# Two loads of v moved in a fused sigmoid attention and gated feed-forward kernel

## The chip, the cores and the metric

The kernel runs on one core of one Trainium2 chip. The metric is device time in microseconds (us) of one execution; the time given is the median of several runs. One further execution is recorded by the hardware profiler, and all views of the profile come from that one.

## The reference

The inputs are q, k and v of shape (8, 12, 448, 64) in float32 (batch, heads, sequence, head dimension), two weights of 768 x 1536 and one of 1536 x 768. Attention uses a sigmoid in place of the softmax, and its output, with heads joined, is the input of a gated feed-forward layer.

```python
scores = scale * np.matmul(q, k.transpose(0, 1, 3, 2)) - np.log(S)
attn = 1.0 / (1.0 + np.exp(-scores))
x = np.matmul(attn, v)                     # then heads joined: (3584, 768)
gate = np.maximum(x @ w_gate, 0.0)
out = (gate * (x @ w_val)) @ w_out
```

## The kernel before

All matrix work is in float16. For each batch the 12 heads are taken as three groups of four (g = 0, 1, 2). A batch passes through these steps:

- *Loads.* `load(b, g0, g1, "kq")` (L106, issued on L110) brings k and q, and `load_v(b)` (L112) brings v, converted from float32 to float16 on the way. They are issued from POOL (GpSimd), which carries out its instructions in order. v is three DMAs: one for the even head pairs (L114) and one for each half of the odd ones (L116), whose partitions are swapped. k and q of a batch have a single buffer (batch 1 has one of its own), v has two that alternate.
- *Transposes of k and q.* Batches 0 and 1 use TensorE (`pe_transposes`). From batch 2 on `dma_transposes(b, g)` (L211) is used: VectorE copies k and q of a group into `rel` (L215), and SyncE issues one DMA transpose from `rel` to `qkT` (L219).
- *Scores.* `qk_unit(b, g, c)` multiplies (L232), and ScalarE applies the sigmoid (L187) into `PT`.
- *pv.* `pv_group(b, g)` multiplies `PT` by v (L250), 28 matmuls for a group; VectorE writes the result to `xT` (L184).
- *Feed-forward.* `gv` forms gate and value for one block f of 128 columns of the two weights (L309), and `down` and `down_pair` multiply by the third weight (L346, L385). From the second half of the kernel on, pairs of batches and blocks are multiplied by a scheme with sums on VectorE and fewer products (`gv_pair`, `down_pair`).

The order on each engine is written out by hand. A loop over the batches (b = 1 to 7) cuts the 21 scores units of a batch into five or six stages (m). Between the scores units of a stage stand the pv groups, and after them a portion of feed-forward work of an earlier batch. Things that are to be issued in the middle of that portion are put in a list `jobs`, in order. So the scores and pv of batch 3 run between feed-forward work of batches 0 to 2, and the pv of a batch's first group is in its third stage (m = 2) from batch 2 on, and in its fourth (m = 3) in batch 1.

`hold(b, g)` (L645) is a copy of two elements of `qkT` on POOL. It computes nothing that is used: POOL can't go on before the DMA transpose (b, g) has landed, so the loads behind it are issued only then. Before the change there are two: on (2, 1), ahead of batch 2's v and the third weight (`late_loads`), and on (3, 2), ahead of batch 4's loads.

The opening loads are in one list (L132 to L160), cut into parts by group and by weight blocks: `load_gv(f0, f1)` loads blocks f0 to f1 - 1 of gate and value weights, one DMA each (L148). A load on POOL waits for the landing of the load eight places ahead of it.

Of the kernel before, what the change touches and what calls it, by code (L numbers as in the profile page):

```python
# [17 lines left out]
def kernel(  # L18
# [75 lines left out]
    def tiles_of(b):  # L94
        if b not in in_tiles:
            pool = early if b == 1 else inp
            in_tiles[b] = tuple(
                p.tile([P, NPAIR, NCH * D], FP16, tag=t, name=t)
                for p, t in ((pool, "k16"), (pool, "q16"), (vinp, "v16"))
            )  # L100
        return in_tiles[b]

    def rows_of(src, b):
        return src[b].rearrange("(x r) (t c) d -> (r t) x (c d)", r=2, c=NCH)

    def load(b, g0, g1, which, c0=0, c1=NCH):  # L106
        for nm, t16, src in zip("kq", tiles_of(b), (k, q)):
            if nm in which:
                xs, cs = slice(2 * g0, 2 * g1), slice(c0 * D, c1 * D)
                nc.gpsimd.dma_start(t16[:, xs, cs], rows_of(src, b)[:, xs, cs])  # L110

    def load_v(b):  # L112
        v16 = tiles_of(b)[2]
        nc.gpsimd.dma_start(v16[:, 0::2, :], rows_of(v, b)[:, 0::2, :])  # L114
        for r in range(2):
            nc.gpsimd.dma_start(  # L116
                v16[64 - 64 * r : P - 64 * r, 1::2, :], rows_of(v, b)[64 * r : 64 * r + 64, 1::2, :]
            )
# [25 lines left out]
    def load_gv(f0, f1, which=(0, 1)):  # L144
        fs = slice(f0 * P, f1 * P)
        for i in which:
            wt, src = ((wg, moe_w_gate), (wv, moe_w_val))[i]
            nc.gpsimd.dma_start(wt[:, :, fs], src[:, fs].rearrange("(c p) f -> p c f", p=P))  # L148
# [6 lines left out]
    load(1, 0, 1, "kq")  # L155
    load_gv(6, 9)
    load(1, 1, 2, "kq")
    load_gv(9, 12)
    load_v(1)
    load(1, 2, 3, "kq")  # L160

    def load_o():
# [27 lines left out]
    def qkT_of(b, g):  # L190
        if (b, g) not in qkT_tiles:
            qkT_tiles[(b, g)] = qkTp.tile([P, TW, P], FP16, tag="qkT", name="qkT")
        return qkT_tiles[(b, g)]
# [17 lines left out]
    def dma_transposes(b, g):  # L211
        k16, q16, _ = in_tiles[b]
        rel = relp.tile([P, TW, P], FP16, tag="rel", name="rel")
        for ti, t16 in enumerate((k16, q16)):
            nc.vector.tensor_copy(  # L215
                rel[:, ti * NCH : (ti + 1) * NCH, :].rearrange("p c (h d) -> p h c d", h=2),
                t16[:, 2 * g : 2 * g + 2, :].rearrange("p h (c d) -> p h c d", c=NCH),
            )
        nc.sync.dma_start_transpose(  # L219
            qkT_of(b, g)[:], rel[:].rearrange("p c x -> p (c x)")  # L220
        )
# [70 lines left out]
    def qk_unit(b, g, c):  # L292
        ps = [bank("qk_ps") for _ in range(2)]
        qk(qkT_tiles[(b, g)], c, 0, NCH, lambda hh: ps[hh][:, 0:S])
        PT = PTp.tile([P, 2, S], FP16, tag="PT", name="PT")
        for hh in range(2):
            sigmoid(PT[:, hh, 0:S], ps[hh][:, 0:S])
        PT_tiles[(b, g, c)] = PT

    def pv_group(b, g):  # L300
        pv(b, g, 0, S, [PT_tiles.pop((b, g, c))[:, :, 0:S] for c in range(NCH)])
# [66 lines left out]
    def open_late():  # L368
        first_sbuf.close()
        pool = ctx.enter_context(tc.tile_pool(name="late", bufs=1))  # L370
        late["T"] = pool.tile([P, 4, HF, HM], FP16, tag="T", name="T")
        late["X"] = pool.tile([P, 3, HD, S], FP16, tag="X", name="X")
        late["sums"] = ctx.enter_context(tc.tile_pool(name="sums", bufs=2))
# [21 lines left out]
    def weight_sums(i):  # L395
        T = [late["T"][:, j] for j in range(4)]
        B11, B21 = wo[:, 0:HF, 0:HM], wo[:, HF:NFC, 0:HM]
        B12, B22 = wo[:, 0:HF, HM:DM], wo[:, HF:NFC, HM:DM]
        sub(T[i], *((B12, B11), (B22, T[0]), (B22, B12), (B21, T[1]))[i])
# [96 lines left out]
    def batch_sums_t1(g):  # L496
        T1, _, _, B11, _, B12, _ = batch_blocks(g, (0, HD))
        sub(T1, B12, B11)

    def batch_sums(g, ks):  # L500
        T1, T2, T4, _, B21, B12, B22 = batch_blocks(g, ks)
        sub(B12, B22, B12)
        sub(T2, B22, T1)
        sub(T4, B21, T2)
# [132 lines left out]
    def pv_finish(b):  # L637
        pv_group(b, NG - 1)
        if b < 2:
            push_gv(b, 0, S, range(NFC))  # L640
# [4 lines left out]
    def hold(b, g):  # L645
        nc.gpsimd.tensor_copy(gate[0:1, :], qkT_tiles[(b, g)][0:1, 0, 0:2])

    def both(b, g):
        pe_transposes(b, g, 0)
        pe_transposes(b, g, 1)  # L650
# [10 lines left out]
    def push_group(g):  # L661
        tail = [("t", g, 6)] + [("y", g, p) for p in range(3)]
        if g == 0:
            tail.insert(0, tail.pop(1))
        work.extend([("w", g, f) for f in range(0, NFC, 2) if g > 0] + tail)
# [26 lines left out]
    for b in range(1, B):  # L692
        if b == 1:
            cuts, pv_at = (0, 3, 6, 9, 13, 17, 21), {3: (0, 2), 5: (1, 2)}
        elif b == 2:
            cuts, pv_at = (0, 4, 7, 11, 14, 18, 21), {0: (-1, 2), 2: (0, 2), 4: (1, 2)}
        else:
            cuts, pv_at = (0, 4, 8, 12, 16, 21), {0: (-1, 2), 2: (0, 2), 4: (1, 2)}
        count = len(cuts) - 1
        hooks = {}  # L700
        if b == 1:
            mix = (3, 3, 3, 3, 3, 2)
            hooks = {
                1: [(1, lambda: both(1, 1))],
                3: [(1, lambda: both(1, 2))],
                4: [(3, lambda: dma_transposes(2, 0))],
                5: [(2, late_loads)],
            }
        elif b == 2:
            mix = (2, 2, 1, 1, 1, 2)  # L710
            hooks = {
                2: [(0, prepare)],
                4: [(0, lambda: weight_sums(0))],
                5: [(1, lambda: weight_sums(1)), (0, lambda: weight_sums(2))],
            }
            open_late()
        elif b == 3:
            mix = (1, 1, 1, 0, 0)
        else:
            mix = (0,) * count  # L720
        for m in range(count):
            jobs = []
            for i, (g, c) in enumerate(order[cuts[m] : cuts[m + 1]]):
                if m in pv_at and i == pv_at[m][1]:
                    if m == 0:
                        pv_finish(b - 1)
                        if b == 2:
                            push_group(0)
                        elif b % 2 == 0:
                            push_group(b // 2 - 1)  # L730
                    else:
                        pv_group(b, pv_at[m][0])
                qk_unit(b, g, c)
            if m == 0 and b > 1:
                jobs.append(lambda: dma_transposes(b, 2))
            if b == 2 and m == count - 1:
                jobs.append(lambda: (dma_transposes(3, 0), dma_transposes(3, 1)))
            elif b == 3 and m == count - 1:
                jobs.append(lambda: (dma_transposes(4, 0), dma_transposes(4, 1)))
            elif 0 <= m - count + 2 and 3 < b < B - 1:  # L740
                jobs.append(lambda: dma_transposes(b + 1, m - count + 2))
            if b == 1:
                if m == 0:
                    load(2, 0, 1, "kq")
                    load(2, 1, 2, "kq")
                    load(2, 2, 3, "kq")
            elif m == 0 and b + 1 < B:
                if b == 3:
                    jobs.append(lambda: hold(3, 2))
                jobs.append(lambda: (load(b + 1, 0, 3, "kq"), load_v(b + 1)))  # L750
            if b % 2 and b > 2:
                if m == count - 1:
                    jobs.append(lambda: (batch_sums_t1(b // 2), batch_sums(b // 2, (0, 1))))
            elif b > 3 and m == 0:
                jobs.append(lambda: batch_sums(b // 2 - 1, (1, HD)))
            if b == 2 and m == count - 1:
                ffn_mix(mix[m], hooks[m])
                next_work(jobs + [lambda: weight_sums(3)], first_act=True)
            elif mix[m]:
                for job in jobs:  # L760
                    job()
                ffn_mix(mix[m], hooks.get(m, ()))
            else:
                next_work(jobs)
            if b == 3 and m in (1, 3):
                for f in range(*((0, 8, 2), (8, NFC, 2))[m // 2]):
                    gate_sums(f, f + 2)
# [35 lines left out]
```

## Time and profile before

| what | value |
|---|---|
| median of 3 runs | 398.85 us (397.96 to 398.97) |
| the profiled execution | 399.14 us |
| its span, first to last instruction | 397.3 us |
| PE (TensorE matmul) busy | 388.5 us, 98% |
| VectorE, ScalarE, POOL busy | 279.6, 223.2, 49.5 us |
| loads from POOL | 23.33 MB on one queue, as written |
| DMA transposes and stores | 19.34 MB on the SyncE queue |

A line of a timeline gives the start of a piece of work and its length in us, the engine, the line of the kernel, the operation with output and input, and how many instructions are merged; in brackets stands the idle time of the engine before it and what ended that. A line of the waits gives the total, the number and the longest. A line of DMA issues gives the size and the median time from issue to landing. A line for a queue gives packets, MB, and the time its packets took as a share of 16 DMA engines in the stretch that was asked for; q0 holds the loads that POOL issues, q1 what SyncE issues.

### The profile page before, as it was taken

The numbers are of one execution on the slowest core, as the hardware profiler recorded it, in microseconds if no ns is written. First come the engines' busy times: TensorE is split into PE (matmuls) and PEld (weight loads), VectorE is DVE, ScalarE is ACT, GpSimd is POOL, SyncE is SP. The second block draws the span as 40 slices with busy tenths as digits, with TensorE's granted clock in tenths as the row PEclk, the third lists the DMA queues.
The fourth block names the chain that finished last, engine by engine and source line by source line (L and its number), as shares of the span: only waits on it lengthen the run. The fifth ranks groups of instructions, "written<-read, shape, count | busy, mean of one in ns | idle before, by whom it ended". The sixth has DMA issues, their size and how long they took to land.

```text
span 397.3 us, 8744 instructions
## 1 busy us (share of the span) xinstructions
PE 388.5 (98%) x3488; PEld 217.5 (55%) x3488; DVE 279.6 (70%) x539; ACT 223.2 (56%) x476; POOL 49.5 (12%) x73
## 2 busy tenths in 40 slices
PE   8999999999999999999999999999999999999995
PEld 3678686445455554554555555455455555555563
DVE  3453345358377889999758889999776779987662
ACT  5946768684785565655665455565566233543121
POOL 8643400700030300003000300000000000000000
PEclk9999999999999999999999999999999999999999
DMA  9999994999999893224945695222013320000135
GB/s 150 196 198 204 206 129 87 180 203 190 203 143 180 167 218 53 46 48 54 177 84 133 130 219 89 48 21 57 19 40 81 81 79 2 0 1 2 40 94 146
DMA packets 68953, 43.69 MB, mean 110 GB/s; under 512 B 35888, under 2 KB 65584, under 8 KB 68912
## 3 DMA queue, kind: packets, MB, share of 16 engines
q0 software_dynamic: 30736, 23.33, 39.2%
q1 hardware_dynamic: 37744, 19.34, 23.2%
q8 instruction: 27, 0.44, 0.4%
q10 hardware_dynamic: 432, 0.46, 0.4%
q14 instruction: 14, 0.11, 0.1%
HBM read 47.19 MB, written 11.01 MB: 146 GB/s over the span
## 4 chain that ended last, share of the span: by engine, by line
PE 84%; DMA 11%; POOL 2%; ACT 1%; issue 0%; DVE 0%; ACTq 0%; POOLq 0%; DVEq 0%
PE u L385 32%; PE g L385 15%; PE y L385 8%; PE qk_ps L232 7%; PE pv_ps L250 7%; PE g_ps L309 5%; PE v_ps L309 5%; DMA wg<-in_moe_w_gate_dram 4%; DMA v<-in_v_dram 3%; PE ya L346 3%; DMA q<-in_q_dram 2%; PE yb L346 1%; DMA qkT<-rel 1%; ACT PT L187 1%; POOL k L110 1%; POOL q L110 1%
## 5 line engine op out<-in xcount | busy, mean ns | idle before, releaser
L187 ACT ACTIVATE PT<-qk_ps 128x448 f16<-128x448 f32 (+3 forms) x318 | 150.5, 595 | 72.6 <-PE qk_ps L232 72.5
L385 PEld LDWEIGHTS <-S 128*128 128x128 f16 x540 | 52.8, 98 | 43.6
L536 DVE TENSOR_TENSOR gsb<-g,gsb 128x448 f32<-128x448 f32 x72 | 42.9, 625 | 14.6 <-PE g L385 14.1
L232 PE MATMUL qk_ps<-qkT 64*64 64x448 f16 (+2 forms) x756 | 49.9, 336 | 1.3 <-DVE qkT L206 0.5
L421 ACT ACTIVATE ysb<-u 128x384 f32<-128x384 f32 x27 | 13.4, 498 | 53.4 <-PE u L385 53.4
L327 DVE TENSOR_TENSOR hT<-gate_sb,v_ps 128x256 f16<-128x256 f32 (+2 forms) x36 | 16.2, 465 | 34.7 <-ACT gate_sb L318 22.3
L532 ACT COPY gsb<-u 128x448 f32<-128x448 f32 x48 | 25.7, 566 | 23.9 <-PE u L385 22.9
L250 PE MATMUL pv_ps<-PT,v 64*64 64x448 f16 (+2 forms) x756 | 37.7, 329 | 1.1 <-DMA v<-in_v_dram 0.8
L184 DVE TENSOR_SCALAR xT<-pv_ps 128x448 f16<-128x448 f32 (+2 forms) x53 | 27.9, 567 | 15.2 <-PE pv_ps L250 13.8
L385 PEld LDWEIGHTS <-hT 128*128 128x128 f16 x288 | 27.7, 98 | 19.8 <-issue 2.1
L232 PEld LDWEIGHTS <-qkT 64*64 64x64 f16 x756 | 20.0, 105 | 25.5 <-issue 16.3
L309 PE MATMUL v_ps<-xT,wv 128*128 128x256 f16 (+2 forms) x216 | 33.3, 290 | 0.3 <-DMA wv<-in_moe_w_val_dram 0.3
L309 PE MATMUL g_ps<-xT,wg 128*128 128x256 f16 (+2 forms) x216 | 33.5, 291 | 0.1
L385 PEld LDWEIGHTS <-wv 128*128 128x128 f16 x216 | 21.1, 98 | 19.7
L385 PEld LDWEIGHTS <-wg 128*128 128x128 f16 x216 | 20.3, 98 | 20.6 <-issue 3.0
L250 PEld LDWEIGHTS <-v 64*64 64x64 f16 x756 | 21.8, 107 | 12.8 <-DMA v<-in_v_dram 1.5
L385 PE MATMUL u<-T,hT 128*128 128x384 f16 x144 | 27.3, 326 | 0.0
L437 DVE SCALAR_TENSOR_TENSOR ysb<-y,ysb 128x384 f32<-128x384 f32 x24 | 13.4, 557 | 17.8 <-PE y L385 10.3
L309 PEld LDWEIGHTS <-wg 128*128 128x128 f16 x216 | 18.5, 98 | 11.5 <-issue 5.0
L110 POOL DMA_DIRECT2D k<-in_k_dram x14 | 10.9, 780 | 110.7 <-DVE rel L215 104.4
L309 PEld LDWEIGHTS <-wv 128*128 128x128 f16 x216 | 20.1, 98 | 7.9 <-DMA wv<-in_moe_w_val_dram 0.6
L385 PE MATMUL u<-xT,wg 128*128 128x448 f16 x108 | 23.5, 353 | 0.1
(69 smaller groups left out, 531.0 us busy)
## 6 DMA issues: line engine op xcount, KB each, us to landing
out_dram<-ysb SPq DMA_DIRECT2D x52, 192.0 KB, 3.0
k<-in_k_dram POOLq DMA_DIRECT2D x5, 672.0 KB, 11.7
q<-in_q_dram POOLq DMA_DIRECT2D x5, 672.0 KB, 14.9
v<-in_v_dram POOLq DMA_DIRECT2D x8, 336.0 KB, 15.4
v<-in_v_dram POOLq DMA_DIRECT2D x16, 168.0 KB, 15.2
k<-in_k_dram POOLq DMA_DIRECT2D x8, 224.0 KB, 10.4
wo<-in_moe_w_out_dram POOLq DMA_DIRECT2D x1, 1536.0 KB, 13.1
q<-in_q_dram POOLq DMA_DIRECT2D x6, 224.0 KB, 11.3
```

The costliest lines, as they stand in the source:

```text
L110: nc.gpsimd.dma_start(t16[:, xs, cs], rows_of(src, b)[:, xs, cs])
L184: nc.vector.tensor_scalar(out=xT, in0=src, scalar1=XSCALE, scalar2=None, op0=AOP.mult)
L187: nc.scalar.activation(PT_ap, ps_ap, AF.Sigmoid, bias=sig_bias, scale=qk_scale)
L232: nc.tensor.matmul(out_of(hh)[o : o + 64, :], qkT[rows, c, cols], qkT[rows, NCH + c0 : NCH + c1, cols], start=True, stop=True, tile_positi ...
L250: nc.tensor.matmul(ps[hh][64 * r : 64 * r + 64, 0:qn], v16[rows, 2 * g + hh, c * D : (c + 1) * D], pieces[c][rows, hh, :], start=(c == 0), ...
L309: nc.tensor.matmul(ps[-1][:, 0:qn], wt[:, dc, f * P : (f + 1) * P], xT_tiles[b][:, dc, q0 : q0 + qn], start=(dc == 0), stop=(dc == NDC - 1),)
L327: nc.vector.tensor_tensor(out=hT_tiles[g][:, f, o : o + qn], in0=gate_sb[:, 0:qn], in1=ps[1][:, 0:qn], op=AOP.mult,)
L346: nc.tensor.matmul(ps[:, 0 : m1 - m0], hT_tiles[g][:, f, t * P : (t + 1) * P], wo[:, f, m0:m1], start=(f == 0), stop=(f == NFC - 1),)
L385: nc.tensor.matmul(ps[:, 0:n], A[:, k_, :], W[:, k_, :], start=(first and k_ == 0), stop=(k_ == kn - 1), skip_group_check=True,)
L421: nc.scalar.activation(o, ps[:, 0:HM], AF.Copy, scale=OUT_SCALE)
L532: by(gs[u][i][:], ps[u][:, 0:S])
L536: nc.vector.tensor_tensor(out=gs[u][i][:], in0=ps[u][:, 0:S], in1=gs[u][i][:], op=AOP.add)
```

## The change

Two loads change place. In the opening list batch 1's v is issued ahead of the gate and value weights of blocks 9 to 11 instead of behind them. Batch 3's v was issued right behind batch 3's k and q, in batch 2's first stage; it is now issued at the end of batch 2's last stage, after the first two DMA transposes of batch 3 and behind a new `hold(3, 1)`. For the later batches v stays behind k and q. No arithmetic changes.

```diff
     load(1, 0, 1, "kq")
     load_gv(6, 9)
     load(1, 1, 2, "kq")
+    load_v(1)
     load_gv(9, 12)
-    load_v(1)
     load(1, 2, 3, "kq")
...
             if b == 2 and m == count - 1:
-                jobs.append(lambda: (dma_transposes(3, 0), dma_transposes(3, 1)))
+                jobs.append(lambda: (dma_transposes(3, 0), dma_transposes(3, 1), hold(3, 1), load_v(3)))
...
             elif m == 0 and b + 1 < B:
                 if b == 3:
                     jobs.append(lambda: hold(3, 2))
-                jobs.append(lambda: (load(b + 1, 0, 3, "kq"), load_v(b + 1)))
+                jobs.append(lambda: (load(b + 1, 0, 3, "kq"), b > 2 and load_v(b + 1)))
```

## The prediction

> **What bounds the kernel now.** I read the page first: PE is busy 98% of the span, all 40 slices of the granted clock read 9, and the chain that ended last is 84% PE. So only time in which PE stands still can be won, and nearly any new PE wait is lost for good. PE's list of waits is next (who waited for what: us in total, times, longest):
>
> ```profile
> PE pv_ps L250 <- DMA v<-in_v_dram: 0.8, 2, 0.5
> PE qk_ps L232 <- DMA qkT<-rel: 0.4, 1, 0.4
> ```
>
> Both places are touched by the change. PE's timeline shows the first, at batch 1's first pv group (start, length, then the idle time in brackets):
>
> ```profile
> 47.18 0.35 PE L250 MATMUL pv_ps<-PT,v 64*64 64x448 f16 x2
> 47.83 0.37 PE L250 MATMUL pv_ps<-PT,v 64*64 64x448 f16 x1 [0.29 <-DMA v<-in_v_dram]
> 48.69 1.51 PE L250 MATMUL pv_ps<-PT,v 64*64 64x448 f16 x25 [0.49 <-DMA v<-in_v_dram]
> 49.85 0.72 PE L232 MATMUL qk_ps<-qkT 64*64 64x448 f16 x8
> ```
>
> The group holds PE from 47.18 to 49.85, 2.67 us; the next such group takes 1.32 in the chain. The wait costs 1.35 us. The second place and the pv group that needs batch 3's v:
>
> ```profile
> 101.36 0.57 PE L232 MATMUL qk_ps<-qkT 64*64 64x448 f16 x8 [0.45 <-DMA qkT<-rel]
> 101.76 1.49 PE L250 MATMUL pv_ps<-PT,v 64*64 64x448 f16 x28
> ...
> 109.47 0.57 PE L232 MATMUL qk_ps<-qkT 64*64 64x448 f16 x8
> 109.88 1.71 PE L250 MATMUL pv_ps<-PT,v 64*64 64x448 f16 x28
> ```
>
> Batch 3's pv starts at 109.88 with no wait, 8.5 us after the transpose wait. Then POOL's timeline, since POOL issues every load in order and its one-element copies (L646) hold it until a transpose has landed:
>
> ```profile
> 69.35 0.17 POOL L646 COPY gate<-qkT 1x2 f16<-1x2 f16 x1 [19.70 <-DMA qkT<-rel]
> 69.83 0.76 POOL L114 DMA_DIRECT2D v<-in_v_dram  x1 [0.31 <-issue]
> 70.58 1.25 POOL L116 DMA_DIRECT2D v<-in_v_dram  x2
> ```
>
> This is batch 2's v behind a hold, the nearest row for what batch 3's v becomes. Asked issue by issue, the DMA view gives time to landing: 5.4 us for each of these, so the last lands at 71.2 + 5.4 = 76.6, 6.8 us after the first issue.
>
> **Part 1, v1 ahead of the last weights.** Nothing is added; five DMAs change order. POOL's waits show that every load waits for the one eight places before it, so the issue slots stay at 26.34, 28.30, 29.44, 30.62 and 34.91. Today weights of blocks 9 to 11 take the first two and v the rest. Landings in that view follow the issue order: the second part of batch 1's q 40.0, wg 42.34, wv 45.2, v 46.9, 47.8 and 48.65. So in the steady stream wg takes 2.3, wv 2.86, v 3.45 us. Swapped: v lands at 40.0 + 3.45 = 43.45, 3.7 us before PE asks. wg lands at 45.8, wv at 48.65. Block 9 reads wg at 51.83 and wv at 52.49 now, so at 50.5 and 51.1 with the wait gone: spare 4.7 and 2.5 us. The k and q loads behind see the same bytes ahead of them; batch 1's last k and q land at 49.7 and 50.9 and are asked for at 51.9 and 52.3. Batch 2's first k and q land at 52.0 and 53.2, against copies at 54.3 and 54.6. ACT idles 1.4 to 1.8 us at 50 and 54, so it is not late next. Part 1 gains **1.35 us**, and all that hangs on PE after it moves forward by as much, the hold at 69.35 and the loads behind it included. From here I keep the clock of before, so this 1.35 is taken off once.
>
> **Part 2, batch 3's transposes without v3 under them.** v3 now lands at 97.4, 98.5 and 99.2, under the transpose issued at 96.75, which takes 4.56 us. The undisturbed ones of this trace take 3.9 to 4.1. With v3 gone it lands at 100.85 and the wait at 101.36 (0.45) goes; next late is PE itself, whose down product ends there anyway. The transposed copies can't start earlier: batch 3's q lands at 95.8, copied at 96.30. Gain **0.45**.
>
> **Part 3, v3 behind the hold.** Added: a hold on the transpose (3,1), 0.17 us of POOL; the three v issues move from 75.63 to behind it. Queued behind on POOL: the hold on (3,2), then batch 4's k, q, v. SP's queue is not reordered, but its next transpose, (3,2), issued at 105.11, now runs beside v3. When does (3,1) land? Now at 99.06 + 4.2 = 103.26. Batch 4's pair, alone, takes from 124.55 to 131.1, 6.55 us; from 96.75 that is 103.3. Same. As at 69.35 the first v issue follows 0.5 us later: **103.85**; the last ends near 105.9. PE asks at 109.88 - 0.45 = **109.43**, so 5.6 us are to be had. Landing has two bounds:
>
> - Alone, 6.8 us (batch 2's v): 110.65, a stall of 1.2.
> - Beside a transpose, bounded by the loads of k that share with one. At 183.8 the two are issued together, and the view answers, beside batch 4's k at 109.86:
>
> ```profile
> k<-in_k_dram POOLq DMA_DIRECT2D x1, 672.0 KB, 11.7
> qkT<-rel SPq DMA_TRANSPOSE x1, 11.5
> ...
> k<-in_k_dram POOLq DMA_DIRECT2D x1, 672.0 KB, 7.1
> ```
>
> k there has v's size (336 + 2 x 168 = 672 KB). The other two shared cases, at 133.6 and 225.3, took 9.9 and 11.8. The queues show why: in the two microseconds from 188 the load queue moved 0.27 MB beside the transpose's, against 0.40 alone from 75:
>
> ```profile
> q0 software_dynamic: 297, 0.27, 91.2%
> q1 hardware_dynamic: 294, 0.08, 40.5%
> ...
> q0 software_dynamic: 453, 0.40, 123.8%
> ```
>
> Which bound? Loads begin to flow 1.8 to 2.1 us after issue, so v3 at 105.8; transpose (3,2), issued at 104.65 by the earlier PE, flows from 105.9. They overlap fully, so the shared rows are the nearest. I take the shortest, 9.9, since only 672 KB run beside the transpose: 113.75, a stall of **4.3 us**; the ends are 1.2 and 115.65 - 109.43 = 6.2. No gain is possible here, as pv doesn't wait for v3 now.
>
> By the Trainium skill, "DMA: Bandwidth & Descriptors", section "Anatomy of one DMA", a load takes about 2.0 us plus its bytes over 436 GB/s. By that, an estimate, 0.69 MB would land 3.6 us after issue, before PE asks, with no stall and a sum of -1.8. The measured 5.4 and 7.1 stand against it, and I go by them.
>
> **What waits behind.** (3,2) lands late too, by 115 at most if it finishes with v3's tail. Its first qk runs at 114.9 + 3.85 = 118.7: free. Batch 4's loads start about 5.4 later (109.86 to 115.3): k lands at 122.4, q at 125.7, v at 129.4. The copies for batch 4 go from 123.80 to 127.65, its first transpose flows from 129.6: free, by little. PE has no slack later that could give the stall back.
>
> **Sum.** -1.35 - 0.45 + 4.3 = +2.5, between -0.6 and +4.4 by the bounds. On the profiled execution (span 397.3, 399.14 in all) that is 401.6; on the median 398.85, which lies 0.3 below it, **401.3**. A difference under 0.3%, 1.2 us, is no change here.
>
> **A clock that drops.** The longest idle of PE after the start is 0.49 us, so no row shows a 4 us one. Bounds from rows: nothing, or what the start shows, where ten 128x448 matmuls took 3.83 us, 0.38 each, against 0.19 later (six in 1.14): 1.9 us. I take nothing, as nearer to all 40 slices at 9, and keep 1.9 for a rival.
> "TensorE: Matmul & The Clock Gate", section "Part 1: The HAM clock gate", says that about 3.4 us of idleness can halve the clock. A 4.3 us stall would pass that mark, and by the rule the sum would be about 1.7 us higher; no row here shows it.
>
> **The rivals.**
> - *Faster: v3 arrives in time.* If (3,1), issued at 98.3 behind the quicker (3,0), lands 4.0 later, at 102.3, and v3 runs as batch 2's did, it lands at 109.65. Only 0.2 of stall is left: -1.6, 397.2. It decides from a landing of v3 before 110.0. For it: the issue of (3,0) takes 2.13 us now, 1.5 elsewhere. Against: the pair at 124.55, and three shared loads. 0.14.
> - *No change: a stall of about 1.2*, v3 ahead of the transpose on the engines. Sum -0.6, 398.3. Against: both flow from 105.8. 0.20.
> - *Part 1 does nothing:* wv, now last, is late at 51.1 instead. It would have to slip by 2.5. Sum +3.85, 402.7. 0.04.
> - *The clock drops* in the stall: +4.4, 403.3. 0.09.
>
> **Numbers.** My forecast has 0.53, of which 0.04 falls within 1.2 us. Slower: 0.49 + 0.04 + 0.09 = 0.62; same 0.20 + 0.04 = 0.24; faster 0.14. The forecast's own range is 399.5 to 403.2. The range for 8 in 10 takes in the no-change rival below and the longest stall above: 398.0 to 403.4.
>
> **What would show it.** Right: no v wait at pv near 47; the qk wait near 101 gone; POOL held until about 102 (all times 1.35 earlier), v issued just behind; a PE wait of 3 to 6 us for v at the pv near 108; shared landings of 9 us or more for v3, and transpose (3,2) above its 4.1. Wrong: landings of v3 under 7 us, a pv there without a wait, a new wait for wv near 51, or one for q or transposes near 128.

## The result, and the profile after

The changed kernel takes 403.63 us (median; 402.76 to 403.67) against 398.77 for the kernel before beside it: ratio 1.0123, 95% interval 1.0107 to 1.0139. It is slower by 4.9 us. The forecast was 401.3 with a range up to 403.4: the direction and the stall came as forecast, the size did not.

The profiled execution took 403.67 us with a span of 401.9. PE's waits in it (total, times, longest):

```profile
PE pv_ps L250 <- DMA v<-in_v_dram: 3.3, 3, 1.6
...
PE pv_ps L250 <- issue: 1.2, 1, 1.2
```

The wait for the transpose (3,0) is gone. The v wait is still there, but it has moved from batch 1 to batch 3. PE's timeline has both places:

```profile
48.23 1.49 PE L250 MATMUL pv_ps<-PT,v 64*64 64x448 f16 x28
49.55 0.55 PE L232 MATMUL qk_ps<-qkT 64*64 64x448 f16 x8
...
100.59 0.57 PE L232 MATMUL qk_ps<-qkT 64*64 64x448 f16 x8
101.00 1.49 PE L250 MATMUL pv_ps<-PT,v 64*64 64x448 f16 x28
...
110.34 0.38 PE L250 MATMUL pv_ps<-PT,v 64*64 64x448 f16 x2 [1.06 <-DMA v<-in_v_dram]
111.41 0.37 PE L250 MATMUL pv_ps<-PT,v 64*64 64x448 f16 x1 [0.69 <-DMA v<-in_v_dram]
113.36 2.81 PE L250 MATMUL pv_ps<-PT,v 64*64 64x448 f16 x25 [1.58 <-DMA v<-in_v_dram]
115.61 0.94 PE L232 MATMUL qk_ps<-qkT 64*64 64x448 f16 x8
116.48 1.31 PE L309 MATMUL g_ps<-xT,wg 128*128 128x448 f16 x6
```

The three waits of batch 3's group are its three DMAs, landing one after another. By the distance of 8.12 us from the pv group ahead of it in the trace of before, this one should have begun at 109.12 and its fourth matmul at 109.27; it ran at 113.36. The stall is **4.1 us**. What comes behind is slow too: the last 25 matmuls and the next eight take 3.12 us to the first g_ps, and 1.82 in a run further down in which the clock held. PE's granted clock, microsecond by microsecond (the column ahead of the last two; 1.00 is full speed, and up to 112 it reads 1.00):

```profile
112.00:113.00 1.00, 0.00 (x0) 0.00 (x0) 0.23 (x1) 0.00 (x0) 0.00 (x0) 0.81 1.29 188
113.00:114.00 1.00, 0.64 (x8) 0.37 (x12) 0.00 (x0) 0.00 (x0) 0.00 (x0) 0.50 0.89 164
114.00:115.00 1.00, 1.00 (x16) 0.50 (x12) 0.00 (x0) 0.00 (x0) 0.18 (x1) 0.50 0.09 16
115.00:116.00 1.00, 1.00 (x20) 0.42 (x13) 0.14 (x1) 0.00 (x0) 0.56 (x1) 0.50 0.03 8
116.00:117.00 1.00, 1.00 (x12) 0.43 (x5) 1.00 (x2) 0.54 (x2) 1.00 (x2) 0.98 0.00 0
```

The clock is halved from 112.6, still inside the stall, to 116.0. From 113.36 on PE has work and does it at half speed for 2.7 us: another **1.3 us**. The chain of waits names where v's time went, from the hold to the landing of the third DMA:

```profile
103.16 0.75 POOL v L114
103.91 0.62 POOL v L116
104.53 8.79 DMA v<-in_v_dram
113.32 0.04 issue
113.36 2.81 PE pv_ps L250 x19
```

From the first issue to the last landing are 10.16 us. And the transpose (3,2) that shares the engines, in SP's timeline, takes 5.26 us to issue where it took 1.55 before the change, and lands 10.0 us after its start, not 4.1:

```profile
104.45 5.26 SPq L219 DMA_TRANSPOSE qkT<-rel  x1
```

PE's place against the trace of before, whose matmuls behind batch 3's first pv start so:

```profile
111.89 1.31 PE L309 MATMUL g_ps<-xT,wg 128*128 128x448 f16 x6
```

Step by step: +1.05 us at batch 1's first pv (the pause near 22 us is longer, 1.15 against 0.27), -0.30 behind it, -0.77 at batch 3's first scores, +4.59 behind batch 3's first pv, and no more after that; the span grew by 4.6.

### The profile page after: what moved, and what is told of

It reads as the page before. It is cut to its first block, busy times and chain, and to the rows that moved or that the text cites. A ratio compares the mean times of both kernels' runs of the same rounds, so it can differ in the third digit from the quotient of the medians.

```text
span 401.9 us, 8747 instructions
## 1 busy us (share of the span) xinstructions
PE 390.6 (97%) x3488; PEld 218.2 (54%) x3488; DVE 279.6 (70%) x539; ACT 223.3 (56%) x476; POOL 49.8 (12%) x74
## 3 DMA queue, kind: packets, MB, share of 16 engines
q0 software_dynamic: 30736, 23.33, 39.5%
## 4 chain that ended last, share of the span: by engine, by line
PE 93%; ACT 3%; DMA 2%; issue 1%; DVE 1%; POOL 0%; ACTq 0%; DVEq 0%
PE u L385 32%; PE g L385 15%; PE y L385 9%; PE qk_ps L232 9%; PE pv_ps L250 8%; PE g_ps L309 7%; PE v_ps L309 6%; PE ya L346 3%; ACT PT L187 2%; DMA v<-in_v_dram 2%; PE warm_ps L175 1%; PE yb L346 1%; PE trt L201 1%; DVE qkT L206 0%; ACT ysb L421 0%
## 5 line engine op out<-in xcount | busy, mean ns | idle before, releaser
L250 PE MATMUL pv_ps<-PT,v 64*64 64x448 f16 (+2 forms) x756 | 39.0, 336 | 4.5 <-DMA v<-in_v_dram 3.3
L110 POOL DMA_DIRECT2D k<-in_k_dram x14 | 10.9, 780 | 110.9 <-DVE rel L215 103.4
```

Of the source, the lines that this page charges most:

```text
L250: nc.tensor.matmul(ps[hh][64 * r : 64 * r + 64, 0:qn], v16[rows, 2 * g + hh, c * D : (c + 1) * D], pieces[c][rows, hh, :], start=(c == 0), ...
```

## The experiments

**The two moves alone.** First batch 1's v only (the edit is to the kernel before):

```diff
+    load_v(1)
     load_gv(9, 12)
-    load_v(1)
```

> Only batch 1's v moves ahead of the weights of blocks 9 to 11; batch 3's v stays where it was. Theory (each part of the change acts by itself): the pv group near 48 no longer waits, 1.35 us less than before, 397.4 us, and the later 0.45 us wait for the transpose (3,0) near 100 stays. Rival (the 1.05 us that the changed kernel's trace lost in its first 47 us belongs to this part): 398.5 us, with PE at the pv group near 48 about 1 us later than before.

Measured: 397.86 against 398.35, ratio 0.9990 (0.9981 to 0.9998). pv has no wait near 48, yet the gain by the ratio is 0.4 us, not 1.35. Then batch 3's v only (the edit is to the changed kernel, as are the edits shown below):

```diff
-    load_v(1)
     load_gv(9, 12)
+    load_v(1)
```

> Only batch 3's v moves behind the hold on (3,1); batch 1's v stays behind the weights. Theory: the 1.35 us wait for v near 48 is back, the transpose wait near 100 is gone, pv of batch 3 waits about 4.1 us and the matmuls behind it run slow for 1.3 us: 398.8 + 4.1 + 1.3 - 0.45 = 403.7 us. If the 1.05 us lost early is not this part's, the pv group near 48 starts at 47.2 as before.

Measured: 403.42 against 398.35, ratio 1.0133 (1.0113 to 1.0152), near the forecast. This move makes the whole loss, and the two ratios multiply to 1.0123, that of the full change. But the wait near 48 did not come back, although batch 1's v stands behind the weights here:

```profile
22.65 0.32 PE L250 MATMUL pv_ps<-PT,v 64*64 64x192 f16 x5 [0.90 <-issue]
47.71 1.49 PE L250 MATMUL pv_ps<-PT,v 64*64 64x448 f16 x28
```

**The kernel before, twice more,** to see how steady that wait is.

> The kernel before, unchanged, for a second trace of it. Theory (the 1.35 us wait for batch 1's v near 48 is one draw of something that varies between executions): the wait lies anywhere between 0 and 1.4 us, and so does the pause that PE has near 22 with no cause shown; 398.4 us. Rival (both belong to the kernel): 1.35 us of wait again, and a pause of 0.3 us near 22.

> The same once more, for a third trace. Theory and rival as for the other repeat; if the waits differ between the three traces the size of the first one says little about the mean.

Measured: 398.30 and 398.65 us. The same place in the two traces, one after the other:

```profile
22.39 0.32 PE L250 MATMUL pv_ps<-PT,v 64*64 64x192 f16 x5 [0.53 <-issue]
47.45 1.66 PE L250 MATMUL pv_ps<-PT,v 64*64 64x448 f16 x28
...
22.67 0.32 PE L250 MATMUL pv_ps<-PT,v 64*64 64x192 f16 x5 [0.70 <-issue]
47.72 1.75 PE L250 MATMUL pv_ps<-PT,v 64*64 64x448 f16 x28
```

The group takes 1.66 and 1.75 us where one without a wait takes 1.49: 0.2 and 0.3 us of wait, not 1.35. The trace on which the forecast rested was an unusual draw: PE came early, at 47.18 after a short pause near 22, and v came late, at 48.65; in the repeats PE comes at 47.45 and 47.72 and v at 47.6 and 47.9. Over all traces the next pv group starts at 59.77 us in the mean with batch 1's v behind the weights (five traces, 59.27 to 60.36) and at 59.38 with it ahead (nine, 59.07 to 59.89). The difference of 0.4 is what the first run of this section measured. The waits themselves say the same: in the five traces they are 1.35, 0.2, 0.3, 0 and 0 us, with pauses near 22 of 0.27, 0.53, 0.70, 0.90 and 1.19 us, so the later PE comes, the less it waits; with v ahead there is none in all nine. What PE waits for near 22 the traces don't show; it varies from 0.3 to 1.2 us over all traces and lies ahead of everything that the change moves.

**The clock.** Sixteen matmuls whose product nobody reads are put into the stall:

```diff
+                        if b == 3 and m == 2:
+                            for _ in range(8):
+                                ps = bank("fill_ps")
+                                for _ in range(2):
+                                    nc.tensor.matmul(ps[:, 0:S], wg[:, 0, 0:P], wg[:, 0, 0:S], start=True, stop=True)
                         pv_group(b, pv_at[m][0])
```

> The changed kernel with sixteen extra 128x448 matmuls on the gate weights, whose product nobody reads, just ahead of batch 3's first pv group, 3 us of TensorE work inside the stall. Theory (the stall lets the clock drop, and that costs 1.3 us beside the stall): v lands as late as before, the clock stays at 1.00, and the time is 1.3 us under the changed kernel, 402.3 us. Rival (the 25 pv matmuls after the stall are slow for another reason, v landing in pieces): no gain, 403.6 us, and the 25 still take over 2 us.

Measured: 402.68 against 398.35, ratio 1.0103 (1.0075 to 1.0132); its interval overlaps that of the changed kernel, so the total alone proves little. The trace does:

```profile
108.21 3.24 PE L736 MATMUL fill_ps<-wg 128*128 128x448 f16 x16
111.38 0.38 PE L250 MATMUL pv_ps<-PT,v 64*64 64x448 f16 x3
112.69 1.51 PE L250 MATMUL pv_ps<-PT,v 64*64 64x448 f16 x25 [0.93 <-DMA v<-in_v_dram]
113.85 0.72 PE L232 MATMUL qk_ps<-qkT 64*64 64x448 f16 x8
114.51 1.31 PE L309 MATMUL g_ps<-xT,wg 128*128 128x448 f16 x6
...
133.47 0.57 PE L232 MATMUL qk_ps<-qkT 64*64 64x448 f16 x8 [1.73 <-DMA qkT<-rel]
```

v is as late as ever (stall 4.4 us), the clock reads 1.00 in every microsecond, and the 25 matmuls take 1.16 us to the next instruction, where the changed kernel needs 2.25. So the 1.3 us are the clock's. In this execution (403.51 us; two others took 401.6 and 401.8) they are given back at 133.47: batch 4's loads wait for the hold on (3,2), which landed 11.9 us after its issue here, and the first transpose of batch 4 then runs beside their end. In the changed kernel PE, slower by the clock, comes there late enough not to wait.

**The sharing.** The transpose (3,2), the hold on it and batch 4's loads move one stage later:

```diff
-            if m == 0 and b > 1:
+            if m == (1 if b == 3 else 0) and b > 1:
...
-            elif m == 0 and b + 1 < B:
+            elif m == (1 if b == 3 else 0) and b + 1 < B:
```

> The changed kernel with the transpose (3,2), the hold on it and batch 4's loads moved one stage later, so that batch 3's v has the engines nearly to itself. Theory (the sharing with the transpose makes v late): v lands 7 to 8 us after its first issue, not 10, pv waits 1 to 2 us, the clock does not drop, 399.7 us (399.2 to 400.2). Rival (the hold itself issues v too late, and sharing does not matter): v still takes about 10 us and the time stays at 403.6.

Measured: 400.57 against 398.35, ratio 1.0063 (1.0043 to 1.0084); the forecast was 0.9 us too low. The transpose is issued 1.65 us later than in the changed kernel, at 106.1. v lands 8.25 us after its first issue, the stall is 2.2 us, and the clock stays at 1.00; the time, the landing and the stall are all a little beyond the ranges that were expected:

```profile
110.95 1.51 PE L250 MATMUL pv_ps<-PT,v 64*64 64x448 f16 x25 [0.49 <-DMA v<-in_v_dram]
```

A wait of 0.81 for batch 4's first transpose takes some back. To take the transpose away altogether, it is issued just ahead of the pv group:

```diff
+                        if b == 3 and m == 2:
+                            dma_transposes(3, 2)
                         pv_group(b, pv_at[m][0])
```

(in place of its issue in stage 0, and with the hold and batch 4's loads in stage 2).

> The changed kernel with the transpose (3,2) issued only just ahead of batch 3's first pv group, near 108.5, and the hold on it and batch 4's loads behind it. Batch 3's v then has the DMA engines to itself but for stores. Theory (sharing with the transpose makes v late, the hold only sets when it starts): v lands 6.5 to 7.2 us after its first issue, the first pv group waits 0.5 to 1.1 us, the clock stays at 1.00; a wait of 0.5 to 2 us for (3,2) or for batch 4's first transpose may come behind; 398.8 to 400.8 us. Rival (v is slow by itself behind a hold): 8 us or more, a pv wait of 2 us or more.

Measured: 406.1 against 398.46, ratio 1.0180 (1.0161 to 1.0199). My expectation failed in the time, in v's landing and in the clock. The transpose waited for its copies, which stood behind other work on VectorE, and was issued at 112.38, after v had landed, so v shared with no transpose; and still:

```profile
102.61 0.74 POOL L114 DMA_DIRECT2D v<-in_v_dram  x1 [0.28 <-PE qk_ps L232]
...
111.49 1.99 PE L250 MATMUL pv_ps<-PT,v 64*64 64x448 f16 x25 [0.43 <-DMA v<-in_v_dram]
```

v took 8.8 us, not 6.5 to 7.2; the rival was right on this. So of the changed kernel's 10.2 us some 1.3 to 2 come from the transpose (10.1 to 10.9 in the runs that share with it from its start, 8.3 to 8.8 in these two), and 2 us over batch 2's 6.8 come from something else. The load queue's figures place these at the end: in the seven microseconds from 104 it moved 0.02, 0.07, 0.15, 0.18, 0.17, 0.07 and 0.02 MB. Batch 2's v began as slowly (0.02, 0.06, 0.20, 0.20 from 71), but the queue then kept its 0.20, with other loads behind v. The output stores move 0.28 MB in the microsecond from 103 and nothing from 105 on, so they do not run beside that slow end. What holds it back stays open. The stall of 2.7 us was enough for the clock:

```profile
112.00:113.00 1.00, 1.00 (x24) 0.53 (x20) 0.32 (x2) 0.00 (x0) 0.00 (x0) 0.69 0.06 16
113.00:114.00 1.00, 1.00 (x13) 0.28 (x5) 0.83 (x2) 0.05 (x1) 0.00 (x0) 0.50 0.42 84
```

The drop comes at 112.38, when PE has already worked again for 0.9 us, and costs about 1.6 us. The rest of the loss in this execution is a wait of 1.9 us for batch 4's first transpose, whose loads started last of all. It took 404.32, the least of the four executions; what the others lost beyond that no trace shows.

So the length of the stall alone does not decide. The clock is at 0.50 for 3.41 us in the changed kernel (112.62 to 116.04) and in this run (112.38 to 115.79), and for 6.83, twice that, in the run with batch 3's v alone (111.91 to 118.73). In every trace here its steps lie a whole number of 3.41 us apart. In the 3.41 us ahead of these three drops PE worked 0.83, 1.64 and 0.87 us; where a wait left the clock alone, it worked 1.93 us or more in each stretch between two instants at which a step could fall. That is no sharp mark, since at the end of the changed kernel a stretch with 1.51 us left it alone too. The price depends on how much of the halved time falls on work: 1.3, 1.6 and 2.4 us in the three.

**An earlier hold.** The new hold waits for (3,0) in place of (3,1):

```diff
-                jobs.append(lambda: (dma_transposes(3, 0), dma_transposes(3, 1), hold(3, 1), load_v(3)))
+                jobs.append(lambda: (dma_transposes(3, 0), dma_transposes(3, 1), hold(3, 0), load_v(3)))
```

> The changed kernel with the new hold on the transpose (3,0) instead of (3,1), so that batch 3's v is issued some 2.1 us earlier, near 101.0, and has a start on the transpose (3,2). Theory (v is late because it is issued 1 us ahead of that transpose and then shares with it): v lands near 109, the pv group near 109.1 waits 0 to 0.6 us, the clock does not drop, and the time is 397.5 to 398.3 us, 5 to 6 us under the changed kernel. Rival (v meets the transpose (3,1) instead and loses there what it gained): v lands near 111, about 399.5 us or more.

Measured: 399.51 against 398.37, ratio 1.0037 (1.0020 to 1.0053): the rival's figure. v is issued at 100.40 as meant, but lands 10.1 us later, and the stall is 2.0 us; the clock holds. One execution of this run took 401.70, and one of the run that moved (3,2) a stage later took 402.43, each some 2 us above the others and with a mean clock of 0.993 against 0.997 to 1.00; the clock may have dropped there, but no trace shows it. With the hold on (3,0) and (3,2) a stage later as well:

> As the run with the hold on (3,0), and the transpose (3,2), its hold and batch 4's loads one stage later. Theory: v lands near 108, no wait of pv; a wait of up to 0.8 us for batch 4's first transpose near 130 can come, as in the run that moved the transpose alone; 397.4 to 398.4 us. Rival (the later loads of batch 4 cost more than the pv wait they save): 399 us or more.

Measured: 399.47, ratio 1.0035 (1.0022 to 1.0048). v lands after 9.1 us and pv still loses 1.0; batch 4's first transpose costs 0.70, so the rival was right here too. Neither of the two holds that were tried is early enough for all 672 KB.

**Half of v.** The even head pairs stay where they were before the change; only the odd halves go behind the hold on (3,0), with batch 1's v ahead of the weights:

```diff
-                jobs.append(lambda: (..., hold(3, 1), load_v(3)))
+                jobs.append(lambda: (..., hold(3, 0), load_v(3, even=False)))
...
-                jobs.append(lambda: (load(b + 1, 0, 3, "kq"), b > 2 and load_v(b + 1)))
+                jobs.append(lambda: (load(b + 1, 0, 3, "kq"), load_v(b + 1, odd=b > 2)))
```

> Batch 1's v ahead of the weights as in the changed kernel; of batch 3's v the even head pairs (336 KB) are loaded where they were before the change, and only the two odd halves (168 KB each) behind a hold on the transpose (3,0). Theory: the even part ends before that transpose flows, so the wait near 100.5 is gone; the odd part is issued near 100.5 and lands by 108, before the pv group near 108.5 asks; 397.4 to 398.0 us, under the kernel before (398.4) and no slower than the run with batch 1's v alone (397.9). Rival (the odd part shares with a transpose and is late): a pv wait of 0.5 us or more and 398.5 us or more.

Measured: 397.83 against 398.46, ratio 0.9983 (0.9974 to 0.9992). The odd halves land near 107, 6 us after issue, and neither the pv group nor the scores ahead of it wait:

```profile
108.88 1.71 PE L251 MATMUL pv_ps<-PT,v 64*64 64x448 f16 x28
```

To see which part brings it, the same with batch 1's v back behind the weights, beside a repeat:

> As the run with batch 3's v in two parts, but batch 1's v back behind the weights, so only the end of the wait for the transpose (3,0) is left as a gain. Theory (the two gains add up, about 0.4 us from batch 1's v and 0.5 from the transpose wait): 0.3 to 0.7 us under the kernel before. Rival (what was gained over the kernel before came from batch 1's v alone): within 0.2 us of the kernel before.

> Batch 1's v ahead of the weights and batch 3's v in two parts, once more beside the run that leaves batch 1's v alone. Theory: 0.5 to 1.0 us under the kernel before, 0.2 to 0.5 under the other run of this pair. Rival: no difference between the two.

Measured: 398.03, ratio 0.9992 (0.9982 to 1.0002), and 397.71, ratio 0.9977 (0.9965 to 0.9988), against 398.36. In both, the waits for the transpose and for v are gone. The first is not told apart from the kernel before. With both parts the time is 0.2% under the kernel before, the lowest median of this study; the interval overlaps that of batch 1's v alone, so what the second part adds is not shown.

## Why the prediction was right or wrong

Two terms of the sum failed: the clock, put at nothing, which cost 1.3 us, and Part 1, put at 1.35 us, which gained 0.4. The stall of Part 3, the largest term, came as forecast.

- *Part 3, the stall:* right. In the clock of before (this trace's times plus 0.30) PE asks at 109.42 (forecast 109.43), v is issued from 103.46 (103.85) and lands at 113.62 (113.75); the stall is 4.1 us, not 4.3. Taking the loads that shared with a transpose as the nearest rows gave the right figure. The reason behind it was half of it: with the transpose out of the way v landed not after 6.8 but after 8.3 to 8.8 us, so no run came near the lower bound on which the no-change and the faster rival rested. That 9.9 came so close to the 10.16 measured is in part luck.
- *The clock:* wrong, the step "I take nothing". No row showed an idle of 4 us, and 40 slices at full clock say nothing on what such an idle does; the first of them reads 9 as well, though ten matmuls there took 0.38 us each. The drop cost 1.3 us here, inside the bounds of 0 and 1.9, and should have stood in the sum as soon as a 4.3 us stall did. The rule of the Trainium skill, "TensorE: Matmul & The Clock Gate", section "Part 1: The HAM clock gate", named the mechanism, and the estimate worked out from it, 1.7 us, was near the price. As the length of a stall its 3.4 us of idleness are no safe mark, though: stalls of 2.0 and 2.2 us left the clock alone, and one of 2.7 us, broken by three matmuls, halved it. In the changed kernel the longest idle time in one piece is 1.58 us.
- *Part 1:* the mechanism was right and the term mis-sized. 1.35 us was read from one execution; the mean gain is 0.4 (0.1 to 0.8 by its interval). No new wait for the weights came, so that rival fell. One landing was misread: the second part of batch 1's q was issued at 24.36 and took 15.1 us, so it landed at 39.5, not 40.0, and wg took 2.9 us, not 2.3. Nothing hangs on it, as v landed at 42.1 in the changed kernel, 6 us before PE asked.
- *Part 2:* right; the wait of 0.45 went, and PE gained 0.47 there.
- *What waits behind:* right for the changed kernel, "free, by little": in five experiments, in which PE or batch 4's loads came at other times, batch 4's first transpose became a wait of 0.3 to 1.9 us.

With the terms as measured, -0.4 - 0.45 + 4.1 + 1.3 = +4.55 against +4.9 on the medians. The stall and the clock's share vary too: the run with batch 3's v alone had 4.8 us of stall and the clock at 0.50 for longer.

## What to carry to other kernels

A load that nobody waits for has its slack in the place where it stands: before it is moved behind a wait, compare the time left from there to its first use (6.0 us here, from v's issue to PE's asking) with the slowest landing of its size, not the fastest. When PE is the bound, a stall of some microseconds can be paid twice, by its length and by the clock behind it. And a wait of about a microsecond, seen in one profiled execution, wants a second trace before it is put into a sum.

## What the runs showed of the hardware

The transpose (3,2), issued while loads ran beside it, kept SP's queue for 2.3 to 6.0 us instead of 1.5 to 1.7, and landed after 5.3 to 11.9 us instead of 3.9 to 4.1. The halved clock outlasted the stall by 2.7 us in the changed kernel, so the time lost is in the matmuls behind the stall and not in any wait that the profile lists. Behind the three stalls that halved it, it stayed halved for 3.41, 3.41 and 6.83 us, after 3.41 us in which PE had worked 0.83, 1.64 and 0.87. By an estimate from the Trainium skill, "DMA: Bandwidth & Descriptors", section "Anatomy of one DMA", v's 0.69 MB, taken as one load, would have landed 3.6 us after issue; 6.8 were measured for batch 2's v and 8.3 to 10.9 for batch 3's. The 0.69 MB are what is written; v is read as float32, 1.38 MB, by which the same estimate gives 5.2 us, nearer to batch 2's but still short of it.
